# Causal products in 64-token blocks, traded halves, and a new list of steps in a linear-attention and Fourier-mixing kernel

## The chip, the core and the metric

The kernel runs on one core of a Trainium2 chip. A core has five engines that run side by side and meet through semaphores: TensorE (PE, matrix products; its weight loads are listed apart as PEld), VectorE (DVE), ScalarE (ACT), GpSimd (POOL) and SyncE (SP), which here issues most DMA transfers. TensorE writes its results to PSUM; the other operands live in SBUF. The metric is the device time of one execution in microseconds; lower is better.

## What is computed

The first part is a gated linear recurrence, for 4 batches of 8 heads, 768 tokens, 48 channels; the second mixes with Fourier transforms and then applies a normalised two-layer network.

```python
f = 1.0 / (1.0 + np.exp(-f_logit))
for t in range(S):
    state = f[:, :, t, :, None] * state + np.einsum('bhd,bhe->bhde', k[:, :, t], v[:, :, t])
    y[:, :, t] = np.einsum('bhd,bhde->bhe', q[:, :, t], state)
...
x = y.transpose(0, 2, 1, 3).reshape(B, S, H * D)
u = x + real(fft(fft(x, axis=1), axis=2))
un = (u - mean(u)) / sqrt(var(u) + 1e-06)
out = u + relu(un @ w_ch1) @ w_ch2
```

Shapes: q, k, v, f_logit are 4 x 8 x 768 x 48; w_ch1 is 384 x 1536, w_ch2 1536 x 384; the output is 4 x 768 x 384.

## The kernel before, in words

**Units.** Two heads of one batch make a unit; there are 16 units, four to a batch. A unit's tiles hold the channels of its two heads on partitions 0 to 47 and 64 to 111, and the 768 tokens along the free side, in six chunks of 128. `attention(u, ...)` is a generator, and each of its steps ends in a `yield`:

1. ScalarE makes the softplus of the gate (L331, L332).
2. VectorE scans it into a running, chunk-wise sum W (L338) and takes the chunk ends (L339); POOL copies one column (L340).
3. ScalarE makes exp(-W) into g, exp(W) into W and the decay of a chunk (L343 to L346).
4. VectorE multiplies q by g (L350) and k into W (L351).
5. TensorE makes the scores of each chunk, 128 keys by 128 queries (`sc`, L362): 24 matmuls, keys in halves of 64 on the two column halves of the array, heads on its two row halves.
6. VectorE copies the causal part of the scores from PSUM into `at` (COPY_PREDICATED, L369), in two halves.
7. In `outputs`: TensorE transposes the weighted keys of five chunks (`st`, L507), ScalarE copies them to kT (L509).
8. TensorE makes the state that each chunk adds (`ds`, L518).
9. VectorE scans the states along the chunks (L526).
10. TensorE multiplies values and scores into y (L538): 12 matmuls with 128 keys as rows, 128 queries wide.
11. TensorE adds what the earlier state gives (L545): ten matmuls. ScalarE copies y into yT in five pieces (L554 to L558).
12. TensorE transposes back (`yt`, L565) and ScalarE copies both heads into x (L567).
13. `fold` prepares the Fourier sums of the batch (L591 to L614), on VectorE and POOL.

**The second part.** When a batch's four units are through, `fnet(b)` makes the Fourier transforms on TensorE (`z` L652, `mix` L671), and `projected(b)` the network: `up` (L752) with w_ch1, ScalarE's ReLU (L754), then products with w_ch2 (`fx`, `fz`, L775), for the first pair of chunks of the first batch a plain product (`po`, L761). The weights are given in 64-bit words; ScalarE, VectorE (L241, L242) and POOL (L243) turn 24 blocks of them into fp32, which is the step `C`, after a load `r`. Near the end `judge` (L824 to L834), the step `M`, forms a flag on VectorE and TensorE that says whether a slower, exact second pass is needed; every engine loads the flag and branches on it. Here the second pass isn't taken.

**What sets the order.** The program is issued in exactly the order of a string of 684 words, `ORDER`. A number is the next step of that unit; F, P and H are steps of the second part by batch; L a load, D a few filler matmuls that write into spare PSUM (`busy`, L154), V and c a second look at the weights for the flag, W a rearrangement of w_ch2, G a memset of a tile's gap rows. Each engine executes its share strictly in that order.

**Buffers.** g and k have three tiles each that units use in turn, q four; W, kT, yT have two. PSUM has one y tile of two banks, two tiles of two banks for scores, transposes and states (`ps_a`), and two of one bank for the second part (`ps_f`).

Of the kernel before, what the change touches and what calls it, by code (L numbers as in the profile page):

```python
# [12 lines left out]
C = 128  # L13
# [5 lines left out]
X_MIN = -24.0  # L19

# [7 lines left out]
    "Gq2 r I D Gq0 L0f Gk1 L1f D Gk0 L0q i D Gq3 C Gq1 Z L0k 0 D 1 Gk2 0 L1q 1 L1k D D D D D D D D D D D "  # L28
    "D 0 0 1 0 r 1 L2f 0 2 C L1v 1 L3fk 1 3 L0v 0 1 L2q 2 0 0 r 1 L2k 3 1 0 2 r 3 L3q 2 L2v 0 C L3v C "
    "L4fk R 4 2 2 3 1 0 C 2 4 1 3 L5qv D L4qv L5fk 3 D D 3 2 0 2 3 2 3 C r 4 1 4 L6fk C r 2 5 4 L6qv 4 2 "  # L30
    "1 5 6 3 4 D 4 C 5 3 T 3 6 4 5 5 4 2 r L7fk 5 2 D L7qv 3 3 5 7 S L8fk C 4 7 6 6 5 F0 5 r r F0 F0 F0 "
    "7 4 C F0 L9fk 5 6 8 H0 H0 6 5 6 r H0 C L8qv 6 7 L9qv P0 6 7 r C P0 7 7 C 9 P0 r r 5 8 C r C F0 r 7 "
    "F0 6 P0 5 9 C 6 7 P0 r C P0 8 8 C P0 r r 7 P0 P0 8 9 H0 C P0 P0 8 7 8 C P0 H0 7 9 6 H0 H0 C 9 r C "
    "P0 9 L10fk r 9 P0 r C 9 L11fk 10 C 6 6 P0 11 4 P0 P0 P0 P0 P0 P0 10 P0 P0 P0 L10qv P0 P0 7 7 F1 9 "
    "P0 F1 H0 9 W P0 P0 P0 11 F1 P0 L11qv P0 P0 P0 9 P0 P0 P0 8 L12fk P0 11 11 8 P0 P0 10 11 F1 P0 11 11 "
    "10 L14fk F1 8 P0 14 F1 P0 10 P0 8 10 P0 P0 H1 H1 10 L12qv P0 P0 10 P0 F1 P0 11 11 10 P0 10 H1 P0 P0 "
    "P0 P0 12 12 12 P0 P0 12 P0 H1 P0 12 P0 H1 L13fk P1 P1 P1 P1 P1 14 13 P1 12 8 8 P1 P1 12 9 10 L13qv "
    "13 P1 P1 L14qv 9 P1 12 11 P1 H1 11 10 P1 P1 13 P1 13 P1 12 P1 P1 14 P1 14 V 13 P1 c V 10 10 P1 P1 "
    "P1 P1 P1 V L15fk P1 13 P1 11 V P1 P1 P1 P1 c P1 11 11 F2 V c F2 F2 H1 13 H1 F2 c 14 P1 c V c P1 P1 "
    "12 P1 P1 14 P1 P1 13 V V V P1 15 F2 c P1 12 P1 P1 P1 P1 c P1 H2 14 15 V V P1 P1 P1 P1 P1 13 P1 14 "  # L40
    "F2 P1 c P1 P1 15 V 13 P1 H2 P1 P1 L15qv P1 14 13 P1 V 12 H2 F2 14 P2 P2 P2 P2 P2 P2 P2 15 P2 P2 P2 "
    "c c 12 H2 V H2 15 H2 15 P2 c P2 15 P2 P2 15 P2 14 13 15 P2 P2 14 P2 P2 15 13 P2 P2 P2 P2 P2 H2 V 15 "
    "P2 P2 14 14 15 H2 P2 P2 P2 P2 15 15 F3 F3 P2 F3 F3 P2 F3 c P2 P2 P2 P2 P2 V P2 c P2 V c c V P2 P2 "
    "P2 P2 P2 c P2 F3 F3 P2 V P2 H3 P2 P2 P2 H3 H3 P2 P2 P2 P2 P2 P2 P2 P2 P2 P2 P3 H3 c P3 P3 P3 P3 V "
    "P3 c P3 P3 P3 c V V c P3 P3 P3 H3 P3 P3 P3 P3 P3 P3 c P3 P3 V P3 H3 P3 P3 P3 P3 P3 P3 H3 H3 P3 P3 "
    "P3 P3 P3 P3 P3 P3 P3 P3 P3 P3 V P3 P3 P3 P3 P3 c P3 c P3 P3 P3 M P3 P3 P3 P3 P3 P3 P3 P3 P3 P3 P3 "
    "P3"
# [7 lines left out]
def kernel(  # L55
# [40 lines left out]
    both = ps_y.tile([128, 2, 512], F32, tag="y", name="y").rearrange("p a b -> p (a b)")  # L96

    y_out, spare = both[:, :S], both[:, S:S + 2 * C]
# [6 lines left out]
    g_t = [fixed([128, S], f"g{i}") for i in range(3)]  # L105
    k_t = [fixed([128, S], f"k{i}") for i in range(3)]
    q_t = [fixed([128, S], f"q{i}") for i in range(4)]
    at_t = [fixed([128, 2, NCH, C], f"at{i}") for i in range(2)]
# [21 lines left out]
    def gap(*tiles):  # L130
        for t in tiles:
            nc.vector.memset(t[32:64], 0.0)

    def start():
# [6 lines left out]
        nc.gpsimd.memset(eps, 1e-6)  # L141
        nc.gpsimd.memset(two, 2.0)
        for t in te_t:
            nc.gpsimd.memset(t, 0.0)
        nc.gpsimd.memset(causal, 1.0)
        nc.gpsimd.affine_select(out=causal, in_=causal, pattern=[[1, C]], compare_op=ALU.is_ge, fill=0.0,
                                base=0, channel_multiplier=-1)

    started = []

    def busy():

        for _ in range(4):
# [823 lines left out]
```

## Time and profile before

| what | value |
|---|---|
| runs | 552.45, 552.56, 554.12 us; median 552.56 |
| profiled execution, first to last instruction | 551.2 us |
| mean granted TensorE clock | 0.982 |
| TensorE's last matmul begins | 544.7 us |
| first `z` matmul begins | 66.3 us |
| fp32 passes of one unit: sc, y at L538, y at L545, ds | 48, 24, 20, 20 |
| COPY_PREDICATED, 32 of 768 elements | 31.3 us on VectorE |
| scan at L338, 16 of them | 28.4 us on VectorE |

The timed runs lie about 1.4 us above the profiled span (552.56 against 551.2); a profiled span runs from the first to the last recorded instruction. Busy time is not the whole of an engine's load: matmul passes overlap each other in the array, so the mean duration of one is its latency, and the distance between starts is what it costs.

### The profile page before, as it was taken

What the parts mean: (1) busy time and instruction counts of PE and PEld (TensorE: products, weight loads), DVE (VectorE), ACT (ScalarE), POOL (GpSimd) and SP (SyncE); (2) the same over time, 40 slices, a digit from 0 to 9 for tenths busy, and PEclk for the clock granted to TensorE, in tenths of its full rate; (3) what the DMA queues carried; (4) which work ended last, traced back from release to release, by engine and by line L of the source; (5) the groups of instructions that cost most, each with busy time, mean ns of one, the idle gap of its engine ahead of it and who ended that gap; (6) DMA issues with size and microseconds to landing.
All of it is one profiled execution on the core that took longest, in us unless ns stands there. A gap on an engine that the chain in (4) does not pass through costs nothing.

```text
span 551.2 us, 10204 instructions
## 1 busy us (share of the span) xinstructions
PE 527.8 (96%) x4186; PEld 463.6 (84%) x4186; DVE 300.1 (54%) x534; ACT 192.8 (35%) x497; POOL 96.1 (17%) x147
## 2 busy tenths in 40 slices
PE   7797989999999999999999999999999999999995
PEld 5686768876898889889889899899889798989985
DVE  8999999984936437426644344444452441413231
ACT  5767485771332432551340422321411303021110
POOL 7146535434001000121101001003001000010000
PEclk9888799999999999999999999999999999999999
DMA  8979745353102100412540301002012004000001
GB/s 220 260 212 227 210 136 165 122 175 107 51 0 73 44 1 7 111 44 84 160 115 17 114 1 59 29 1 87 0 30 87 1 14 159 0 30 0 30 2 34
DMA packets 18398, 44.38 MB, mean 81 GB/s; under 512 B 3109, under 2 KB 4710, under 8 KB 18342
## 3 DMA queue, kind: packets, MB, share of 16 engines
q1 hardware_dynamic: 17094, 39.89, 25.9%
q0 software_dynamic: 1104, 3.54, 1.8%
q8 instruction: 35, 0.57, 0.4%
q10 hardware_dynamic: 144, 0.20, 0.1%
q14 instruction: 21, 0.17, 0.1%
HBM read 38.90 MB, written 4.72 MB: 79 GB/s over the span
## 4 chain that ended last, share of the span: by engine, by line
PE 88%; DVE 3%; ACT 3%; DMA 2%; POOL 1%; issue 1%; SPq 0%; ACTq 0%; POOLq 0%
PE up L752 35%; PE fx L775 16%; PE fz L775 12%; PE y L538 4%; PE sc L362 3%; PE z L652 3%; PE y L545 3%; PE po L761 3%; PE mix L671 3%; PE ds L518 2%; PE yt L565 2%; PE st L507 1%; PE pt L710 1%; DMA k<-in_qkf_dram 1%; DMA g<-in_qkf_dram 1%
## 5 line engine op out<-in xcount | busy, mean ns | idle before, releaser
L752 PE MATMUL up<-unT,w 128*128 128x256 f32 x864 | 197.0, 382 | 1.5 <-DVE x L730 0.9
L752 PEld LDWEIGHTS up<-unT,w 128*128 128x128 f32 x864 | 161.0, 190 | 26.1 <-issue 1.5
L754 ACT ACTIVATE h<-up 128x256 f32<-128x256 f32 x144 | 55.2, 383 | 199.4 <-PE up L752 199.4
L619 POOL DMA_INDIRECT out_dram<-x,place x16 | 16.9, 1056 | 270.4 <-DVE x L805 234.0
L775 PE MATMUL fx<-block,h 128*128 128x192 f32 x264 | 46.5, 326 | 0.0
L775 PE MATMUL fx<-w,h 128*128 128x192 f32 x264 | 44.9, 327 | 0.1
L775 PEld LDWEIGHTS fx<-w,h 128*128 128x128 f32 x264 | 43.1, 190 | 0.8 <-ACT h L754 0.4
L775 PEld LDWEIGHTS fx<-block,h 128*128 128x128 f32 x264 | 43.5, 190 | 0.0
L782 DVE TENSOR_TENSOR s<-h,h 128x768 f32<-128x768 f32 x11 | 10.5, 954 | 50.3 <-ACT h L754 50.3
L243 POOL TENSOR_TENSOR w<-w,raw 128x384 uint32<-128x384 uint32 x24 | 28.2, 1178 | 45.8 <-ACT raw L239 25.6
L369 DVE COPY_PREDICATED at<-causal,sc 128x768 f32<-128x768 uint32 x32 | 31.3, 1031 | 0.9 <-PE sc L362 0.8
L362 PE MATMUL sc<-q,W 48*64 48x128 f32 x768 | 26.3, 283 | 5.2 <-issue 3.3
L362 PEld LDWEIGHTS sc<-q,W 48*64 48x64 f32 x768 | 22.1, 138 | 8.9 <-issue 5.4
L338 DVE TENSOR_TENSOR_SCAN W<-g,bound 112x768 f32<-112x768 f32 x16 | 28.4, 1775 | 0.8 <-issue 0.7
L727 DVE TENSOR_TENSOR x<-mix,x 128x384 f32<-128x384 f32 x12 | 6.7, 555 | 39.0 <-PE mix L671 39.0
L538 PE MATMUL y<-at,v 128*64 128x128 f32 (+1 forms) x384 | 27.9, 300 | 0.0
L538 PEld LDWEIGHTS y<-at,v 128*64 128x64 f32 (+1 forms) x384 | 23.9, 143 | 3.2 <-issue 3.2
L775 PE MATMUL fz<-w,s 128*128 128x192 f32 x132 | 23.5, 328 | 0.0
L775 PE MATMUL fz<-block,h 128*128 128x192 f32 x132 | 23.5, 328 | 0.0
L775 PE MATMUL fz<-w,h 128*128 128x192 f32 x132 | 23.4, 327 | 0.0
L775 PEld LDWEIGHTS fz<-w,s 128*128 128x128 f32 x132 | 21.6, 190 | 0.3 <-issue 0.3
L697 ACT ACTIVATE rstd<-mv,eps 128x1 f32<-128x1 f32 (+1 forms) x20 | 5.9, 294 | 45.7 <-DVE mv L694 45.7
(145 smaller groups left out, 750.3 us busy)
## 6 DMA issues: line engine op xcount, KB each, us to landing
raw<-in_w_ch_dram SPq DMA_DIRECT2D x24, 384.0 KB, 4.3
g<-in_qkf_dram SPq DMA_DIRECT2D x32, 144.0 KB, 4.4
q<-in_qkf_dram SPq DMA_DIRECT2D x32, 144.0 KB, 4.1
k<-in_qkf_dram SPq DMA_DIRECT2D x32, 144.0 KB, 4.7
v<-in_v_dram SPq DMA_DIRECT2D x16, 288.0 KB, 5.0
k<-in_w_ch_dram SPq DMA_DIRECT2D x12, 384.0 KB
g<-in_w_ch_dram SPq DMA_DIRECT2D x12, 384.0 KB, 5.2
out_dram<-x SPq DMA_DIRECT2D x4, 168.0 KB
```

The costliest lines, as they stand in the source:

```text
L243: nc.gpsimd.tensor_tensor(bits, bits, lo, ALU.add)
L338: nc.vector.tensor_tensor_scan(W, g, bound[:R], 0.0, ALU.add, ALU.min)
L362: nc.tensor.matmul(ps[64 * s:64 * s + 64, r, i * C:(i + 1) * C], lhsT=W[ROWS[r], o + 64 * s:o + 64 * s + 64], rhs=Q[ROWS[r], o:o + C], sta ...
L369: nc.vector.copy_predicated(AT[:, :, half], causal.bitcast(U32).unsqueeze(1).unsqueeze(1).to_broadcast([128, 2, NCH // 2, C]), ps[:, :, :N ...
L538: nc.tensor.matmul(y[FILL[r], c * C:(c + 1) * C], lhsT=vt[:, c, r * D:r * D + (64 if r == 0 else D)], rhs=AT[:, r, c], start=(c % 4 == 0), ...
L545: nc.tensor.matmul(y[ROWS[r], c * C:(c + 1) * C], lhsT=st[ROWS[r], :, c - 1], rhs=Q[ROWS[r], c * C:(c + 1) * C], start=False, stop=True, s ...
L619: nc.gpsimd.indirect_dma_start(out=out.rearrange("b s d -> (b s) d"), out_offset=bass.IndirectOffsetOnAxis(ap=place[:, b, i:i + 1], axis=0 ...
L652: nc.tensor.matmul(z[:, cols], lhsT=src[:, j, lo:hi], rhs=tab[:, t, T % 2, cols], start=(i == 0), stop=(i == len(parts) - 1), skip_group_c ...
L671: nc.tensor.matmul(mix[:, o], lhsT=zz[:rows_of[T], T, PLACES[c]], rhs=cd[:rows_of[T], T, :NQ - odd], start=(i == 0), stop=(i == 1))
L752: nc.tensor.matmul(pp[:, :256], lhsT=w1[:, kt, m * 128:(m + 1) * 128], rhs=unT[:, kt], start=(kt == 0), stop=(kt == 2))
L754: nc.scalar.activation(hs[-1][:, m % H].rearrange("p t n -> p (t n)"), pp[:, :256], AF.Relu)
L775: nc.tensor.matmul(out, lhsT=h[:, m], rhs=blocks[i][:, m], start=(start and m == 0), stop=(m == H - 1), skip_group_check=True)
```

## The change

Scores are no longer made as 128 x 128 blocks. A chunk's causal products are split into 64-token blocks: `own`, the two diagonal blocks (each key half with its own queries), and `far`, the first key half with the second half's queries, which needs no mask. The masked copy covers the diagonal blocks alone, in one instruction; ScalarE copies `far`. The weighted keys go into g instead of W, so g lives longer and has four tiles instead of three, and the gap rows of k are set to 2^20 so that the product in the gap stays usable for the next unit. For chunks 3 to 5 the two key halves change places (in `swap`, and in the load of v, now three transfers), and for chunks 0 to 2 the two heads change places in y (`into`), so that matmuls that follow each other take the four quadrants of the array and write to different banks. y lies in two banks, three chunks in each. The keys' transposes become a step of their own, `K`. The value products come in three parts: the second diagonal block before `far`, the other two before the states. The list of steps is new.

```diff
-    y_out, spare = both[:, :S], both[:, S:S + 2 * C]
+    y_out = ps_y.tile([128, 2, 512], F32, tag="y", name="y")
+    spare = y_out[:, 0, 3 * C:]
...
-    g_t = [fixed([128, S], f"g{i}") for i in range(3)]
+    g_t = [fixed([128, S], f"g{i}") for i in range(4)]
...
-    at_t = [fixed([128, 2, NCH, C], f"at{i}") for i in range(2)]
+    at_t = [fixed([128, 2, NCH, 64], f"at{i}") for i in range(2)]
+    ao_t = [fixed([128, 2, NCH // 2, 64], f"ao{i}") for i in range(2)]
...
-        for _ in range(4):
-            nc.tensor.matmul(spare, lhsT=bound[:, :C], rhs=bound[:, :2 * C], start=not started, stop=True,
+        for _ in range(8):
+            nc.tensor.matmul(spare, lhsT=bound[:, :C], rhs=bound[:, :C], start=not started, stop=True,
...
+                nc.sync.dma_start(out=v_of[u][:, :3], in_=v[b, hp, :, :3])
+                for s in range(2):
+                    nc.sync.dma_start(out=v_of[u][64 * s:64 * s + 64, 3:],
+                                      in_=v[b, hp, 64 - 64 * s:128 - 64 * s, 3:])
...
-        nc.vector.tensor_tensor(W, W, K, ALU.mult)
-        yield
-
-        scores = []
-        for h in range(2):
-            ps = ps_a.tile([128, 2, 512], F32, tag="sc", name=f"sc{u}_{h}")
...
-                        nc.tensor.matmul(ps[64 * s:64 * s + 64, r, i * C:(i + 1) * C],
-                                         lhsT=W[ROWS[r], o + 64 * s:o + 64 * s + 64],
-                                         rhs=Q[ROWS[r], o:o + C], start=True, stop=True)
...
+        swap = lambda a: a[:, 3 * C:].rearrange("p (c s t) -> p c s t", c=3, s=2)
+        nc.vector.tensor_tensor(g[:, :3 * C], W[:, :3 * C], K[:, :3 * C], ALU.mult)
+        nc.vector.tensor_tensor(swap(g)[:, :, ::-1], swap(W), swap(K), ALU.mult)
+        yield
+
+        own = ps_a.tile([128, 2, 512], F32, tag="sc", name=f"sc{u}_0")
+        for c in range(NCH):
+            for s in range(2):
+                o, k = c * C + 64 * s, c * C + (64 * s if c < 3 else 64 - 64 * s)
+                for r in range(2):
+                    nc.tensor.matmul(own[64 * s:64 * s + 64, r, c * 64:c * 64 + 64], lhsT=g[ROWS[r], o:o + 64],
+                                     rhs=Q[ROWS[r], k:k + 64], start=True, stop=True)
+        yield
+
+        nc.vector.copy_predicated(
+            AT, causal[:, :64].bitcast(U32).unsqueeze(1).unsqueeze(1).to_broadcast([128, 2, NCH, 64]),
+            own[:, :, :NCH * 64].rearrange("p r (c t) -> p r c t", t=64))
...
+        into = lambda c, r: 1 - r if c < 3 else r
+        def values(c, r, rows, t, weights):
...
+            nc.tensor.matmul(y[FILL[g], c // 3, c % 3 * C + t.start:c % 3 * C + t.stop],
+                             lhsT=vf[rows, o:o + (64 if g == 0 else D)], rhs=weights,
+                             start=new, stop=True, skip_group_check=True)
...
+            halves(hi, lo, hi, lambda p, r, c: own[p, r, c])
+            ps = ps_a.tile([128, 2, 512], F32, tag="sc", name=f"sc{u}_1")
...
+            nc.scalar.copy(far, ps[:, :, :NCH // 2 * 64].rearrange("p r (c t) -> p r c t", t=64))
+            yield
...
+            halves(lo, hi, hi, lambda p, r, c: far[p, r, c % 3])
+            halves(lo, hi, lo, lambda p, r, c: own[p, r, c])
...
-        for c in range(1, NCH):
-            for r in range(2):
-                nc.tensor.matmul(y[ROWS[r], c * C:(c + 1) * C], lhsT=st[ROWS[r], :, c - 1],
+        for c, r in ((1, 0), (4, 1), (4, 0), (1, 1), (2, 0), (3, 1), (3, 0), (2, 1), (5, 0), (5, 1)):
+            nc.tensor.matmul(y[ROWS[into(c, r)], c // 3, c % 3 * C:c % 3 * C + C], lhsT=st[ROWS[r], :, c - 1],
...
-        nc.scalar.copy(
-            x[:, :, hp * 2 * D:(hp + 1) * 2 * D].rearrange("t c (r e) -> t c r e", r=2),
-            ps[:, :NCH * 128].rearrange("t (c r k) -> t c r k", r=2, k=64)[:, :, :, :D])
+        nc.scalar.copy(x_to[:, :3], heads[:, :3, ::-1])
+        nc.scalar.copy(x_to[:, 3:], heads[:, 3:])
```

In the list, the first F0 stood behind 153 words and stands behind 136; before it came nine C and now seven, and units 6 and 7, which had done four and two steps there, have not begun. The last word before was the last P3, with M twelve words ahead of it; now M is the last word.

```diff
-    "P3 P3 P3 P3 P3 P3 P3 P3 P3 P3 V P3 P3 P3 P3 P3 c P3 c P3 P3 P3 M P3 P3 P3 P3 P3 P3 P3 P3 P3 P3 P3 "
-    "P3"
+    "P3 P3 V P3 P3 P3 P3 P3 P3 P3 c c P3 P3 P3 P3 V P3 P3 P3 P3 P3 P3 P3 P3 c P3 P3 P3 P3 P3 P3 M"
```

## The prediction

> **What bounds the kernel now.** I read the page first, then the clock of the core, the busy time by stretch, TensorE's groups by shape, the chain of waits, and last the order in which TensorE's and VectorE's instructions stand in both programs.
>
> ```profile
> span 551.2 us, 10204 instructions
> ...
> PE 527.8 (96%) x4186; PEld 463.6 (84%) x4186; DVE 300.1 (54%) x534; ACT 192.8 (35%) x497; POOL 96.1 (17%) x147
> ...
> DVE  8999999984936437426644344444452441413231
> ...
> DMA  8979745353102100412540301002012004000001
> ...
> PE 88%; DVE 3%; ACT 3%; DMA 2%; POOL 1%; issue 1%; SPq 0%; ACTq 0%; POOLq 0%
> ```
>
> 88% of the chain is TensorE, but the DVE row says that the first ninth or more of the run is another stage: its tenths are 9 for eight slices of 13.8 us. The stretches, cut where the first `z` matmul starts (66.31), where the last weight word is converted on VectorE (123.6) and at TensorE's last matmul (545.1), make it sharp:
>
> ```profile
> 0.00:66.31 66.31, 53.51 (x766) 45.27 (x766) 61.09 (x88) 41.41 (x81) 32.94 (x65) 0.87 0.87 225
> 66.31:123.60 57.29, 54.85 (x585) 43.70 (x585) 53.90 (x91) 41.17 (x107) 26.15 (x28) 1.00 0.53 155
> 123.60:545.10 421.50, 419.41 (x2837) 374.66 (x2835) 184.59 (x358) 110.19 (x311) 36.99 (x55) 1.00 0.16 48
> 545.10:551.20 6.10, 0.00 (x0) 0.00 (x0) 0.52 (x1) 0.00 (x0) 0.00 (x0) 0.79 0.22 74
> ```
>
> Columns: stretch, length, PE, PEld, DVE, ACT, POOL busy, granted clock, DMA share, GB/s. Stage one: VectorE busy 61.1 of 66.3 us, loads 0.87 of the DMA engines. Stage two: VectorE 53.9 of 57.3 and TensorE 54.9, both full. Stage three: TensorE alone. Then 6.1 us of tail. Of stage three's matmuls the change touches these:
>
> ```profile
> L538 PE MATMUL y<-at,v 128*64 128x128 f32 x192 | 27.6, 300 | 0.0
> L538 PE MATMUL y<-at,v 128*48 128x128 f32 x192 | 27.4, 299 | 0.0
> L362 PE MATMUL sc<-q,W 48*64 48x128 f32 x768 | 26.3, 283 | 5.2 <-issue 3.3 <-DVE at L369 1.3 <-PE yt L565 0.4
> ...
> L545 PE MATMUL y<-q,stt 48*48 48x128 f32 x320 | 21.4, 277 | 0.0
> ```
>
> Every fp32 matmul shows as two passes, so x768 is 384 matmuls. The mean of one is its latency; what counts is the rhythm of starts:
>
> ```profile
> 184.43 0.38 PE L752 MATMUL up<-unT,w 128*128 128x256 f32 x1
> 184.74 1.54 PE L362 MATMUL sc<-q,W 48*64 48x128 f32 x48
> 186.21 0.48 PE L752 MATMUL up<-unT,w 128*128 128x256 f32 x1
> ```
>
> One unit's 48 `sc` passes own 1.47 us. The single start times inside show four passes beginning within 20 ns, one per quadrant of the array, and the next four 109 ns later: 12 x 0.109 = 1.31, and 0.16 goes into entering and leaving the small mode. The `up` burst behind it takes 1.49 us for 6 passes instead of 1.30, another 0.19 for coming back. Read the same way, `y` at L538 runs in twos (12 x 0.109 + 0.15 = 1.45), `y` at L545 also in twos (10 x 0.109 + 0.16 = 1.27), `ds` takes 0.78.
>
> **What the skill says.** (1) "TensorEngine Tiling (Array Packing)", Key Properties: changing the tiling mode drains the engine, and tiles load and multiply in parallel. The trace agrees: 0.16 + 0.19 us per excursion, four starts in 20 ns. (2) "TensorE: Matmul & The Clock Gate", LDWEIGHTS: the load takes its columns / 1.2 ns, 53 ns for 64. In `ds` (48 moving columns) the two column groups run independently, one start every 45 ns with 48 weight columns and every 58 ns with 64: the weight load sets the pace, plus 5 ns. (3) The same page, "Wait — 56ns, not 53.3ns?": starts never average closer than about 25 ns however short the matmul. The trace neither shows nor excludes that: `sc` averages 27 ns, `ds` 25. In favour of the change: TensorE's sequencer stood in a wait until 27.97 us and reached its next wait at 28.72, and handed over 48 passes between them, 15.7 ns each.
>
> **The change, part by part.** *Causal products.* Before, 24 `sc` + 12 `y` matmuls of 128 columns. After, per unit: 24 `own`, 12 `far` and 36 value matmuls of 64 columns, all in quadrants. No row shows such a pass. Bounds for a group of four: 56 ns (streaming, half of 109 plus the fixed part) and 109 ns (no gain from halving). I take 60: the 58 of `ds`, with the sequencer's 4 x 15.7 = 63 behind a partly filled queue. *Between chunks (L545).* "Halves traded" puts heads of chunks 0 to 2 on the other column group, so ten matmuls run in fours and a last two: 6 x 0.109 = 0.65 for 1.09. Quadrants running in fours at 128 columns are exactly what `sc` shows, so this has one answer.
>
> I count by the two orders from the first `z` on. Before: 240 sc x 0.0545 + 132 y x 0.109 + 110 y x 0.109 = 39.5 us. After: 240 own + 396 value + 132 far = 768 x 0.030 = 23.0, plus 120 x 0.0654 = 7.8, plus 10 more `ds` 0.6: 31.5. Gain 8.0. Mode changes: before 44 in x 0.163, 45 out x 0.19, 2 between small modes x 0.15 (80 ns drain and a 53 ns load laid bare) = 16.0; after 34, 33 and 13 (values to `ds`): 13.8. Gain 2.2. `up`, `fx`, `fz`, `z`, `mix`, `po` keep their counts and shapes. Together TensorE's work from the first `z` falls by **10.2 us**.
>
> *VectorE.* One COPY_PREDICATED of 768 elements (1.03 us) per unit instead of two; W*k (1.05) becomes two halves of about 0.55. Up to the subtraction that feeds the first `z`, summing mean durations in issue order gives 64.5 us before and 52.6 after: 12 predicated copies become 5 (-7.2), one scan fewer (-1.8), two weight blocks later (-2.0), the rest small. Up to the last weight word 120.7 and 108.1: 20 copies become 9 (-11.3). In the trace these points fall at 65.3 and 123.6, so sum and clock agree. Against it: in the first 20 us the new order has fewer fillers, and VectorE stands behind `own` and behind the exponentials; I charge 2.5 us. The first `z` starts at 66.3 - 11.9 + 2.5 = 57, and stage two keeps its length, since work of both engines there falls together. Loads: about 10.7 MB have to be in by then (six units of 1.18, seven blocks of 0.39, tables), at 225 GB/s 48 us plus 4.5 to landing, so they fit with 5 us to spare; `v` in three transfers instead of one costs SP two issues of 0.4 us per unit on a queue that is not full.
>
> *ScalarE.* A `far` copy (384 elements, 0.49 by the `unT` row) and heads copied in two (0.64 becomes 2 x 0.40): 0.65 us per unit. ACT's sum at the first `z` is 43 us, beneath VectorE's 53, so it is hidden; but the second value step waits for the `far` copy, and in the new order often only 0.7 us of TensorE work lies between, against 0.1 + 0.49 + 0.1, with a 0.38 `h` activation perhaps ahead of it. TensorE and all queued there wait: nothing to 0.5 us for each of 11 units; I take 2 us. The one y tile is held longer, from the first value step to the last yT copy (1.5 us); from the seventh unit on 2.7 to 15 us of TensorE work lies between, so no cost; were that cover gone, each unit would wait up to 1.5. A fourth g tile costs POOL one more memset (0.73) ahead of `bound`, which is then ready near 4.6 us, before the first scan at about 6. Keys' transposes as an own step are the same five instructions; filler matmuls, half as long and twice as many, sit where TensorE idles; the kept gap value changes no instruction.
>
> *The tail.* The judging step moves from twelve steps ahead of the end to the very end. Before, its flag was there at 526.3, and the end was set by ScalarE's last store, its flag load (0.48) and 2.45 us from its branch to its next instruction. After, from TensorE's last matmul: 0.6 the last sum, 0.98 six small VectorE instructions, 0.45 the matmul, 0.45 two more: flag at +2.5. Then POOL's flag load and branch 0.63, 2.6 until it goes on, 2.46 for its closing instructions (1.47 of it one drain), 0.8 teardown: 9.0 instead of 6.2, **+2.8**. If the drain isn't fixed, +1; at least 0.
>
> Sum: -9.3 (start) - 10.2 + 2.0 + 2.8 = -14.7 on a span of 551.2. The median of the runs lies 1.4 above the span: 552.6 - 14.7 = **538 us**.
>
> **Rivals.** *Start-up doesn't move as far:* loads or the order's latency hold the first `z` at 64 to 65. For it, DMA at 0.87; against it, VectorE was the fuller one. 538 + 7.5 = 545.5. *Better than the sum:* the tail hidden, no waits for `far`, no filler lack: 538 - 2.8 - 2.0 - 2.5 = 531. *The other side:* short passes don't start faster than the long ones, because a floor of about 25 ns per start, or weight loads of two quadrants in turn, holds a group of four at 109 ns. Then 768 x 0.0245 = +18.8: 557 us, slower. It decides from a group of 98 ns on (14.7 / 768 = 0.019 per matmul). Against it stand the sequencer's 15.7 ns and the independent rhythms in `ds`. *The change doesn't do what it says* (values not in four quadrants, banks in conflict): L545 already shows two row groups writing one bank on different partitions without delay; it would give about 550.
>
> **Chances.** The sum 0.58, start-up held 0.17, better 0.14, slower 0.08, about even 0.03. The range 529 to 548 holds the first three with their spread. A measurement tells about 0.3% (1.7 us): faster 0.90, same 0.02, slower 0.08.
>
> **What would show it.** `own` bursts of 48 passes at about 0.9 us, L545's successor at 0.8; a first `z` near 57; the last weight block near 113; the stretch from the first `z` to the last matmul about 8 us shorter than 478.8; a tail of 9. It is wrong if groups of four come every 100 ns, if the first `z` stays near 65, or if TensorE shows new idle time in stage three.

## The result, and the profile after

The changed kernel takes 549.12 us (median of 8 runs, 542.71 to 549.97), the kernel before 552.91 in the same series: a ratio of 0.9896, 95% interval 0.9858 to 0.9933. It is faster by 1%, where 2.6% had been forecast. The runs of the changed kernel lie in two groups, three at 542.7 to 544.4 us and five at 548.8 to 550.0; the profiled run, 549.43 us with a span of 547.7, belongs to the second.

From the page of the changed kernel: span, TensorE's row, VectorE's, the clock's and the DMA engines' tenths in 40 slices, and the shares of the chain that ended last.

```profile
span 547.7 us, 12758 instructions
...
PE 516.5 (94%) x5422; PEld 456.8 (83%) x5422; DVE 292.4 (53%) x534; ACT 200.3 (37%) x529; POOL 99.2 (18%) x149
...
DVE  7859889996754265564354356143264730514141
...
PEclk9888599999999999999999999999999999999997
DMA  7994657776100301213010323202010021120101
...
PE 70%; DVE 5%; POOL 1%; DMA 1%; issue 1%; ACT 0%; DVEq 0%; POOLq 0%
```

TensorE makes 5422 passes instead of 4186. Its share of the chain, 70% against 88% before, can't be compared: this chain could be followed back only to 111.9 us, the one before to 0.8. VectorE's row, which began with an 8 and seven 9s, now holds a 7, an 8 and a 5 in its first three slices, and the clock's row three 8s and a 5 in its first five. The stretches of the changed kernel, cut at the same events as before (first `z` at 65.02, last weight word on VectorE at 125.4, TensorE's last product at 537.32; columns: length, then busy time of PE, PEld, DVE, ACT, POOL, granted clock, DMA share, GB/s):

```profile
0.00:65.02 65.02, 51.67 (x1170) 44.34 (x1171) 51.41 (x79) 40.45 (x83) 29.52 (x60) 0.80 0.79 186
65.02:125.40 60.38, 56.02 (x937) 44.65 (x936) 56.50 (x95) 44.32 (x117) 26.89 (x31) 0.99 0.71 191
125.40:537.32 411.92, 408.46 (x3316) 367.72 (x3315) 182.71 (x353) 115.52 (x330) 42.77 (x59) 1.00 0.16 50
537.32:547.70 10.38, 0.38 (x2) 0.09 (x2) 1.77 (x9) 0.00 (x0) 0.00 (x0) 0.67 0.14 47
```

Start-up is where the gain is missing. VectorE's busy time fell by 9.7 us (61.09 to 51.41), but the stretch became only 1.3 us shorter, because VectorE's time without work rose from 5.2 (66.31 - 61.09) to 13.6 (65.02 - 51.41). TensorE has 1170 matmul passes in it instead of 766, at a clock of 0.80 instead of 0.87. What VectorE waited for in this stretch:

```profile
DVE stt L573 <- PE ds L565: 3.5, 1, 3.5
DVE q L359 <- ACT g L352: 2.1, 1, 2.1
DVE at L374 <- PE sc L370: 1.9, 3, 1.0
```

(Total us, times, longest.) In the kernel before no gap in front of VectorE was longer than 0.84 us from 2 us to the first `z`; its longest there:

```profile
DVE eo L593 <- POOL eo L591: 0.8, 1, 0.8
```

The three gaps of the changed kernel lie at 26.4 to 29.9, 35.7 to 37.8 and, for the longest of the third, 40.5 to 41.5 us.

The short passes themselves behave. A burst in the steady part of the changed kernel (start, length, passes):

```profile
195.23 0.57 PE L528 MATMUL y<-at,v 64*48 64x64 f32 x24
195.60 0.55 PE L545 MATMUL sc<-q,g 48*64 48x64 f32 x24
195.95 0.90 PE L370 MATMUL sc<-q,g 48*64 48x64 f32 x48
```

From start to start 24 passes take 0.37 and 0.35 us: 6 groups of four at about 60 ns.

### The profile page after: what moved, and what is told of

It reads as the page before. It is cut to its first block, busy times and chain, and to the rows that moved or that the text cites. A ratio compares the mean times of both kernels' runs of the same rounds, so it can differ in the third digit from the quotient of the medians.

```text
span 547.7 us, 12758 instructions
## 1 busy us (share of the span) xinstructions
PE 516.5 (94%) x5422; PEld 456.8 (83%) x5422; DVE 292.4 (53%) x534; ACT 200.3 (37%) x529; POOL 99.2 (18%) x149
## 4 chain that ended last, share of the span: by engine, by line
PE 70%; DVE 5%; POOL 1%; DMA 1%; issue 1%; ACT 0%; DVEq 0%; POOLq 0%
PE up L791 29%; PE fx L814 16%; PE fz L814 12%; PE z L691 3%; PE mix L710 2%; PE y L528 2%; PE pt L749 1%; PE y L582 1%; DMA raw<-in_w_ch_dram 1%; PE yt L602 1%; PE po L800 1%; PE ds L565 1%; PE sc L370 1%; PE st L507 1%; DVE w L251 1%
## 5 line engine op out<-in xcount | busy, mean ns | idle before, releaser
L374 DVE COPY_PREDICATED at<-causal,sc 128x768 f32<-128x768 uint32 x16 | 16.6, 1040 | 18.8 <-PE sc L370 18.6
L750 ACT COPY unT<-pt 128x384 f32<-128x384 f32 x24 | 11.5, 483 | 30.3 <-PE pt L749 30.3
L528 PE MATMUL y<-at,v 64*48 64x64 f32 (+1 forms) x768 | 19.6, 235 | 2.5 <-DVE at L374 1.5
L359 DVE TENSOR_TENSOR q<-q,g 112x768 f32<-112x768 f32 x16 | 16.9, 1054 | 9.5 <-ACT g L352 9.5
L814 PEld LDWEIGHTS fz<-block,h 128*128 128x128 f32 x132 | 21.7, 190 | 0.3 <-PE fx L814 0.3
L349 POOL COPY deep<-W 112x1 f32<-112x1 f32 x16 | 5.5, 344 | 89.7 <-DVE W L347 89.7
L814 PEld LDWEIGHTS fz<-w,h 128*128 128x128 f32 x132 | 21.7, 190 | 0.0
L814 PEld LDWEIGHTS fz<-w,s 128*128 128x128 f32 x132 | 21.7, 190 | 0.0
```

The lines of the kernel that those rows point to most:

```text
L359: nc.vector.tensor_tensor(Q, Q, g, ALU.mult)
L374: nc.vector.copy_predicated(AT, causal[:, :64].bitcast(U32).unsqueeze(1).unsqueeze(1).to_broadcast([128, 2, NCH, 64]), own[:, :, :NCH * 64 ...
L528: nc.tensor.matmul(y[FILL[g], c // 3, c % 3 * C + t.start:c % 3 * C + t.stop], lhsT=vf[rows, o:o + (64 if g == 0 else D)], rhs=weights, st ...
L750: nc.scalar.copy(turned[j][:, :, t], pt[:, :DM].rearrange("p (k t) -> p k t", k=3))
L814: nc.tensor.matmul(out, lhsT=h[:, m], rhs=blocks[i][:, m], start=(start and m == 0), stop=(m == H - 1), skip_group_check=True)
```

## Experiments

Three places were open: the tail (10.4 us, before 6.2), the start-up, and what makes VectorE wait there. Theories for the wait: the loads (v in three transfers with smaller packets), the clock (half for 27 us before 66 instead of 17), the fetching of TensorE's instructions, and the order with its one y tile.

| kernel | median us | ratio to before, 95% interval | first z | VectorE without work before it |
|---|---|---|---|---|
| changed | 549.12 | 0.9858 to 0.9933 | 65.0 | 13.6 |
| e1 judge early | 549.93 | 0.9905 to 0.9946 | 65.8 | 14.4 |
| e2 v in one transfer | 550.54 | 0.9927 to 0.9964 | 67.8 | 16.7 |
| e3 more filler | 548.82 | 0.9881 to 0.9935 | 65.7 | 14.7 |
| e4 fewer filler instructions | 549.10 | 0.9897 to 0.9944 | 65.2 | 13.7 |
| e5 long products, units 0 to 3 | 550.03 | 0.9909 to 0.9959 | 64.0 | 7.5 |
| e6 before, small fillers | 553.96 | 0.9989 to 1.0025 | 67.3 | 6.3 |
| e7 judge among up | 545.59 | 0.9804 to 0.9885 | 64.7 | 13.7 |
| e8 fewer loads | 549.38 | 0.9899 to 0.9949 | 66.5 | 15.6 |
| e9 fewer value passes | 547.31 | 0.9875 to 0.9918 | 61.5 | 9.3 |
| e10 long products and judge | 547.06 | 0.9863 to 0.9910 | 65.6 | 8.7 |
| e11 judge, filler at 18 us | 547.44 | 0.9836 to 0.9893 | 61.8 | 10.8 |
| e12 judge, long products in two units | 542.97 | 0.9764 to 0.9810 | 62.3 | 9.5 |
| e13 before, halved in four units | 559.50 | 1.0086 to 1.0155 | 68.8 | 7.8 |
| e14 before, halved in all | 560.28 | 1.0080 to 1.0149 | 77.3 | 12.2 |

The last two columns are from the profiled run of each, the medians from all its runs (4 to 22); in the kernel before they are 66.3 and 5.2. The kernels were timed in several series, in which the kernel before took 552.7 to 555.0 us, so kernels of different series are compared by the ratio. One profile tells the start-up to about 1 us: the changed kernel, e1 and e7 have the same list up to the first `z`, which begins at 65.0, 65.8 and 64.7.

### The tail: e1 and e7

e1 moves M right behind the last `c`, the size step of the look at the weights:

```diff
-P3 P3 P3 c P3 P3 P3 P3 P3 P3 M
+P3 P3 P3 c M P3 P3 P3 P3 P3 P3
```

> The changed kernel with the judging step M put right behind the last size step, ahead of the last six steps of the last network, instead of at the very end. Theory (the tail after the last matmul is set by the flag and the engines' jump behind it): the 10.4 us from TensorE's last matmul to the end fall to 6 to 7, as in the kernel before (6.2), and the time falls by 3.5 to 4 us, with the first z where it was (65.0). Rival (the tail is the stores and the closing work of the engines, whatever M does): within 1 us of the changed kernel.

The tail fell to 6.3 us, as the theory had it, and the time stayed. TensorE lost it ahead of the end: its stretch from the first `z` to the last product is 477.1 us long instead of 472.3. Its waits from 500 us on in e1:

```profile
PE turned L870 <- DVE most L868: 2.7, 1, 2.7
PE fz L814 <- DVE most L871: 0.4, 1, 0.4
```

Behind them the granted clock was at half from 531.6 to 535.0 us. The judging matmul waits for six VectorE instructions, which stand behind the size step and behind sums that need TensorE's own last products. So e7 puts all of it among `up` matmuls, whose results go to ScalarE:

```diff
-V P3 P3 P3 P3 P3 P3 P3 c c P3 P3 P3 P3 V P3 P3 P3 P3 P3 P3 P3 P3 c P3 P3 P3 P3 P3 P3 M
+V V P3 P3 P3 P3 P3 P3 P3 c c P3 P3 c P3 P3 P3 P3 M P3 P3 P3 P3 P3 P3 P3 P3 P3 P3 P3 P3
```

> The changed kernel with the last load and size step eight steps earlier and the judging step twelve steps ahead of the end, as far from it as in the kernel before, among matmuls with w_ch1, whose results go to ScalarE. Theory (judging early costs TensorE only where VectorE is needed by the products around it): tail near 6.3, no standstill before it, 3.5 to 4 us less than the changed kernel. Rival: TensorE stands 2 to 3 us ahead of the judging matmul here too, and the time is that of the changed kernel within 1 us.

The last stretch of e7:

```profile
538.13:544.60 6.47, 0.00 (x1) 0.00 (x0) 0.56 (x1) 0.00 (x0) 0.00 (x0) 0.84 0.21 71
```

From 500 us on TensorE's only wait is 0.2 us, and the tail is 6.5 us instead of 10.4: judging last costs the changed kernel about 4 us in its profile. The median is 3.5 us lower (545.59 to 549.12, ratios 0.9845 to 0.9896), but the intervals of the two overlap. The pair e5 and e10 below, which differ in the same edit, is 3.0 us apart (ratios 0.9934 and 0.9886), and its intervals just touch.

### Loads: e2 and e8

e2 lays v out in DRAM with the halves already traded:

```diff
-                nc.sync.dma_start(out=v_of[u][:, :3], in_=v[b, hp, :, :3])
-                for s in range(2):
-                    nc.sync.dma_start(out=v_of[u][64 * s:64 * s + 64, 3:],
-                                      in_=v[b, hp, 64 - 64 * s:128 - 64 * s, 3:])
+                nc.sync.dma_start(out=v_of[u], in_=v[b, hp])
```

> The changed kernel with v laid out in DRAM with the key halves of chunks 3 to 5 already traded, so that each unit's v is one transfer with packets of 2304 bytes instead of three with packets of 1152. Loads theory (smaller packets and two more issues per unit slow the start-up): first z from 65.0 to 61 or earlier, DMA rate in the first 40 us from about 210 to about 240 GB/s, time 3 to 4 us less. Clock, fetch and order theories: first z moves by less than 1.5 us and the time by less than 1.5 us.

The DMA rate of the first 40 us rose only from 210 to 219 GB/s, and the first `z` came later, at 67.8. e8 leaves out the loads of v for units 2 to 5, about a quarter of what is loaded before the first `z`; these units use the v of units 0 and 1:

```diff
             if name == "v":
+                if 2 <= u < 6:
+                    v_of[u] = kept[u % 2]
+                    continue
```

> The changed kernel with the loads of v for units 2 to 5 left out (2.4 MB of about 10; those units use v of units 0 and 1, so their share of the output is another). Fetch theory as to its second half (the fetches come late because the DMA engines are full): TensorE's standstills near 20.6, 33.6 and 46.6 us shrink to under half, and the first z comes 2 to 4 us earlier. Rival (the standstills are the same with freer DMA engines): they stay at 1.3 to 2 us, and the first z moves by less than 1 us.

The first standstill shrank from 1.38 to 0.17 us, the second grew to 2.48, and the first `z` came at 66.5. The loads of v as the limit are out: neither larger packets nor fewer bytes brought VectorE its work sooner. The order of the other loads was not tested; in the changed kernel ScalarE waits 1.5 us for a gate's load until 21.7 us, and VectorE 0.7 us in its wake. That full DMA engines make the standstills is not shown either.

### Clock: e3 and e11

e3 adds nine `D` words where TensorE waits between 44 and 62 us (`C 4` becomes `C D D D D 4`, the others singly or in pairs ahead of `3`, `5`, `K4`, `K5`).

> The changed kernel with nine more filler groups between 44 and 62 us, where TensorE waits for VectorE ahead of own, inter and the keys' transposes. Clock theory (TensorE's gaps bring the granted clock to half, and the half clock delays what VectorE waits for): the half clock of 49.3 to 66.4 shrinks to at most 7 us and the first z comes 2 to 4 us earlier. Loads, fetch and order theories: the clock may rise, but the first z stays within 1 us of 65.0, since VectorE is busy 0.85 of that stretch anyway.

The half clock from 49.3 to 66.4 us was gone; in the 66 us it fell from 27 to 10 us. The first stretch of e3:

```profile
0.00:65.69 65.69, 50.25 (x1242) 44.09 (x1243) 51.01 (x79) 40.21 (x83) 29.10 (x59) 0.92 0.75 184
```

Clock 0.92 instead of 0.80, first `z` no earlier. There VectorE is full, and a slow TensorE costs nothing. But from 23.2 to 30.1 us the clock was at half in e3 too, and there VectorE waits for TensorE. e11, on top of e7, adds three `D` words at that place:

```diff
-1 2 L1v D 3 0 K1
+1 2 L1v D D D D 3 0 K1
```

> The kernel with the early judging (last load and size step eight steps earlier, judging twelve steps ahead of the end) and three more filler groups between the own products of unit 1 and the inter-chunk products of unit 0, near 20 us. Clock theory for the first large gap of VectorE (26 to 30 us; it is there in all profiles whose clock is at half for 3.4 us or more between 22 and 30, and small where it isn't): the clock stays full until 33 us, the gap shrinks from 3.9 to under 2 us, first z 1 to 2 us earlier than 64.7. Rival (that gap is the number of passes ahead of ds): the gap stays over 3 us, or grows by the 1.3 us of the fillers, whatever the clock.

The clock stayed full until 47 us, and the first `z` came at 61.8, 3.0 us earlier than in e7. The gap named in the expectation shrank less than the theory said, from 3.9 to 2.8 us; the later ones at 36 and 41 us shrank from 2.9 to 1.5 together. So the fillers there are worth some 3 us of start-up in these two profiles. Not all of that need be the clock: a standstill of TensorE near 33 us, of a kind that the next runs deal with, was 0.3 us long in e11 and 1.8 in e7. The time didn't follow (547.44 against 545.59, with overlapping intervals): in the profiled run the stretch from the first `z` to the last product took 478.4 us instead of 473.4. At its place, TensorE's timeline in e11:

```profile
121.63 0.67 PE L565 MATMUL ds<-v,kT 128*64 128x48 f32 x15
125.15 0.41 PE L565 MATMUL ds<-v,kT 128*48 128x48 f32 x5 [2.86 <-issue]
```

A burst of 20 passes breaks off for 2.86 us and goes on; "issue" means that it waited for nothing that the profile shows. The clock then fell to half from 125.9 to 129.3. What such a break is, the next runs show.

### Instructions: e4, e6, e5, e9, e13, e14

The changed kernel breaks off in the same way, between two passes of one burst that have the same operands ready:

```profile
20.25 0.46 PE L582 MATMUL y<-q,stt 48*48 48x128 f32 x4
22.09 0.68 PE L582 MATMUL y<-q,stt 48*48 48x128 f32 x8 [1.38 <-issue]
```

Queue q8 of the DMA part carries instructions, 44 packets of 16 KB in the changed kernel and 35 in the kernel before. They fit TensorE's program: its 10,844 and 8,372 records (weight loads and passes) in groups of 256 would make 42 and 33. One packet was moved from 19.2 to 20.5 us, 1.56 us before the burst went on. e4 makes the filler groups of fewer instructions:

```diff
-        for _ in range(8):
-            nc.tensor.matmul(spare, lhsT=bound[:, :C], rhs=bound[:, :C], start=not started, stop=True,
+        for _ in range(2):
+            nc.tensor.matmul(spare, lhsT=bound.bitcast(F32)[:, :C], rhs=bound.bitcast(F32)[:, :C],
+                             start=not started, stop=True,
```

> The changed kernel with each filler group as two fp32 matmuls of 128 columns instead of eight bf16 ones: about the same TensorE time, half of the fillers' instructions (some 100 fewer before 13 us). Fetch theory (TensorE's instruction fetches, 16 KB for about 256 instructions, come late when the DMA engines are full, and TensorE stands in the middle of bursts at 20.7, 33.6 and 47 us): these standstills move later or vanish, the half clock behind the first one vanishes with it, and the first z moves by 1 to 3 us, probably earlier. Loads and order theories: the first z stays within 1 us of 65.0.

The first `z` stayed (65.2), so as a cure it failed, but the break moved, to another instruction of the program:

```profile
17.91 0.61 PE L566 MATMUL ds<-v,kT 128*64 128x48 f32 x13
19.91 0.46 PE L566 MATMUL ds<-v,kT 128*64 128x48 f32 x7 [1.40 <-issue]
```

The clock was full until 37.7 us here, and VectorE's gap at 26 us shrank to 0.6 and 1.1 us in two pieces; but a break of 3.2 us at 33.8 us is followed by gaps of 1.4 and 3.0 us, at 36.9 and 39.0.

That gave the means to test it. Counting TensorE's records up to a break, and looking for the instruction packet ahead of it, for ten of the breaks in the first 50 us:

```
kernel    record (mod 256)   stands from..to    after the packet's end
changed   698 (186)          20.71..22.09       1.56
changed   1205 (181)         33.55..34.88       1.56
e2        954 (186)          28.29..29.55       1.50
e4        445 (189)          18.51..19.91       1.46
e4        950 (182)          28.51..29.22       1.38
e4        1205 (181)         33.81..37.01       1.58
e7        698 (186)          20.58..22.01       1.56
e7        1459 (179)         40.27..40.87       1.53
e11       698 (186)          20.76..22.14       1.44
e11       1461 (181)         36.66..37.47       1.59
```

The breaks sit at one place modulo 256, give or take some records that are missing from a trace, and so do all others of 0.2 us or more in the first 50 us of the changed kernel, e1 to e4, e7, e8 and e11 (178 to 187). That holds whatever instruction stands there: record 698 is an inter-chunk product in the changed kernel and a filler in e11, and in e4, with fewer filler records ahead, the boundaries fall into `ds` and into the next unit's `own`. The Trainium skill ("Trainium Architecture — The Big Picture", The software stack) gives 64 bytes for an instruction; 16,384 / 64 = 256 agrees with the distance of the breaks. A break lasts until about 1.5 us after the packet of the next 256 instructions has been moved, which takes 0.9 to 1.4 us.

e6 is the counter-test with instructions where TensorE has time to spare, in the kernel before:

```diff
-        for _ in range(4):
-            nc.tensor.matmul(spare, lhsT=bound[:, :C], rhs=bound[:, :2 * C], start=not started, stop=True,
+        for _ in range(16):
+            nc.tensor.matmul(spare[:64, :64], lhsT=bound[:, :64], rhs=bound[:, :64], start=not started, stop=True,
```

> The kernel before with each filler group as sixteen bf16 matmuls of 64 weight and 64 moving columns instead of four of 128 and 256: about the same TensorE time, four times the fillers' instructions. Fetch theory: TensorE now stands in front of instruction fetches in the first 45 us, for 1 us or more at a time, each standstill ending about 1.5 us after a 16 KB fetch; the first z comes 1 to 3 us later. Rival (instruction supply doesn't limit TensorE): the first z within 0.5 us of 66.3 and no standstill that ends so.

The theory lost here: no break at such a place, VectorE's idle time up by 1.1 us, the median the same within its interval. More instructions where TensorE has time to spare do no harm. That leaves the dense bursts. e5 takes the old products for units 0 to 3, in the new list, in which only K0 to K3 move, each behind the next step of its unit:

```diff
+        if u < 4:
+            yield from long_products(u, x_all, Q, K, W, te)
+            return
         swap = lambda a: a[:, 3 * C:].rearrange("p (c s t) -> p c s t", c=3, s=2)
...
-        if te is None:
-            keys_turned(u, K)
+        if te is None or long:
+            if te is None:
+                keys_turned(u, K)
             for c in range(NCH):
```

> The changed kernel in which units 0 to 3 make their products as the kernel before did (24 sc of 128 queries, 12 value matmuls of 128 keys, two masked copies), in the new list, with v still in three transfers; a unit then has 72 fp32 passes there instead of 144, so half the instructions; units 4 to 15 are those of the changed kernel. Fetch theory (many short passes use up the fetched instructions faster than full DMA engines bring new ones): TensorE's standstills of 1.3 to 2 us at 20.7, 33.6 and 46.5 us vanish, and the first z comes at 58 to 61, although VectorE has four more masked copies (4.1 us). Order theory (the new list and the one y tile chain the units): the first z stays at 65 or comes later, by up to 4 us for the added copies, with VectorE's gaps still there.

VectorE's gaps between 20 and 45 us fell from 7.2 to 0.8 us, in nearly the new list and with the one y tile. That speaks against the order as the cause, but doesn't rule it out: VectorE's busy time rose from 51.4 to 56.5 us by the added masked copies and slower products, which fills gaps too, and the first `z` came at 64.0 only, between the two expectations. e9 keeps VectorE's and ScalarE's work and takes only value passes away:

```diff
-            halves(hi, lo, hi, lambda p, r, c: own[p, r, c])
+            if u >= 4:
+                halves(hi, lo, hi, lambda p, r, c: own[p, r, c])
...
+            else:
+                for c in range(NCH):
+                    for r in range(2):
+                        values(c, r, slice(0, C), slice(0, C), own[:, r, min(c, 4):min(c, 4) + 2])
+                for p, c in ((lo, 0), (hi, 3)):
+                    for r in range(2):
+                        values(c, r, p, hi, far[p, r, 0])
```

> The changed kernel in which units 0 to 3 form their values with 12 matmuls of 128 keys and 128 columns and 4 short ones instead of 36 short ones (the columns come from the own blocks of two chunks, so these units' share of the output is another): about the same TensorE time, the same work on VectorE, ScalarE and the DMA queues, 104 fp32 passes per unit instead of 144. Fetch theory: fewer and shorter standstills, VectorE's gaps between 20 and 42 us shrink from 8.6 to 5 us or less, and the first z comes at 60 to 62. Rival (the length of the chain from own to inter, with the one y tile, sets it): VectorE's gaps stay near 8 us and the first z within 1 us of 65.0.

First `z` at 61.5, inside the expected 60 to 62. VectorE's waits before it in e9, and the stretch:

```profile
DVE stt L582 <- PE ds L574: 3.0, 1, 3.0
DVE q L132 <- PEq L1013: 1.0, 1, 1.0
DVE at L374 <- PE sc L370: 0.8, 1, 0.8
```

```profile
0.00:61.45 61.45, 50.07 (x1011) 43.23 (x1011) 52.17 (x79) 39.90 (x83) 30.00 (x59) 0.86 0.77 196
```

The gap behind ScalarE's `g` (2.1 us) is gone; that at `ds` remains with 3.0, from 25.6 to 28.6 us, and the clock is at half from 23.6 to 27.0. No break at the boundary is left. So the largest gap needs no break: at half clock, with short passes still in front of `ds`, most of it stays. Fewer instructions are one thing that e9 changes; it also lets the first value step start later. e13 removes that doubt: the kernel before, with the same operands, waits and list, only each product of the first four units made as two halves:

```diff
+                w = C if u >= 4 else 64
+                for n in range(0, C, w):
...
-                        nc.tensor.matmul(ps[64 * s:64 * s + 64, r, i * C:(i + 1) * C],
+                            nc.tensor.matmul(ps[64 * s:64 * s + 64, r, i * C + n:i * C + n + w],
                                          lhsT=W[ROWS[r], o + 64 * s:o + 64 * s + 64],
-                                         rhs=Q[ROWS[r], o:o + C], start=True, stop=True)
+                                             rhs=Q[ROWS[r], o + n:o + n + w], start=True, stop=True)
```

> The kernel before, in which units 0 to 3 make each sc and each value matmul as two of 64 columns instead of one of 128, with the same operands, buffers, waits and list: 144 fp32 passes per unit for these two instead of 72, as the changed kernel has, at nearly the same TensorE time (a group of four at 58 instead of 2 x 54.5 per pair: sc 1.4 us instead of 1.3). Instruction theory (twice the instructions in the first units make TensorE stand for fetches and slow VectorE's chain): standstills of TensorE at indices near 185 modulo 256 of its instruction count appear before 45 us, VectorE's idle time before the first z grows from 5.2 us by 2 to 5 us, and the first z moves from 66.3 to 68 to 71. Rival (the extra instructions are free; the loss of the changed kernel comes from its order, its far step or its one y tile): the first z stays within 1 us of 66.3.

It became slower by 1.2% (559.50 us, interval 1.0086 to 1.0155). TensorE's and VectorE's waits in its first 50 us, the first break, and the stretch before the first `z`:

```profile
PE sc L364 <- issue: 4.3, 2, 3.0
...
PE y L542 <- issue: 3.0, 2, 1.6
...
DVE at L371 <- PE sc L364: 3.2, 2, 3.0
```

```profile
16.79 0.88 PE L364 MATMUL sc<-q,W 48*64 48x64 f32 x30
20.71 0.71 PE L364 MATMUL sc<-q,W 48*64 48x64 f32 x17 [3.04 <-issue]
```

```profile
0.00:68.81 68.81, 52.93 (x1054) 45.55 (x1055) 60.99 (x87) 40.93 (x80) 32.02 (x63) 0.90 0.86 214
```

Breaks at records 445, 698 and 952 (189, 186, 184 modulo 256), of 3.04, 1.58 and 1.43 us, ending 1.70, 1.58 and 1.35 us after their packets: the place modulo 256 that the breaks of the changed kernel have, in a kernel that had no break there. (The other 1.3 us of the `sc` row, ahead of 48.1 us, are no break: they stand in front of the first pass of a burst, whose W VectorE had just written, and the kernel before has 1.8 and 1.5 us of this kind, ahead of 28.0 and 44.7 us.) The first one begins at 17.67 and its packet at 17.7 us, so here the next instructions were not fetched ahead. VectorE stood from 18.9 to 22.0 us in its wake, its time without work rose by 2.6 us (5.2 to 7.8) while its busy time stayed (61.1 to 61.0), and the first `z` moved by 2.5 us to 68.8. So it is shown that TensorE breaks off for its instructions and that VectorE stands for it. How much of the 8.4 us in the changed kernel is this, no run shows: e13 has 2.6 of it. Nor is all of e13's loss in start-up: its profile is 5.1 us longer than that of the kernel before, and 2.2 of these lie between the first `z` and the last weight word, with a clock of 0.97 instead of 1.00, which stays unexplained.

e14 does the same in all units (the bound `u >= 4` becomes `u >= 16`).

> The same halving in all 16 units. Instruction theory: as with four units up to the first z; behind it the fetches are covered where bursts of short passes stand between long ones, so the stretch from the first z to the last matmul grows from 478.7 by at most 4 us (12 units times some 0.15 us of longer bursts, and a standstill here or there). If instruction supply limits TensorE there too, it grows by 8 us or more.

The median is that of e13 within 0.8 us, and the stretch behind the first `z` takes 480.5 us in its profile against 481.1 in e13: halving the other twelve units costs nothing there that can be told. Its profiled run, with the first `z` at 77.3, was its slowest (566.13 us); the first 77 us are read no further.

### The best version: e10 and e12

e10 joins e5 and e7, e12 does so with long products in units 0 and 1 alone (`if u < 2`).

> The two edits of long products in units 0 to 3 and of judging twelve steps ahead of the end together. If they add up: first z near 64, tail near 6.3, and the time of the kernel with the early judging alone or up to 1 us less. If the long products give nothing in the median, the time is 545 to 546.

> The early judging, and long products in units 0 and 1 alone, so two more masked copies on VectorE (2.1 us) than the changed kernel and half the instructions for the first two units. If the early gap comes from the short passes of units 0 and 1 and each unit pays its own share: the gap at 26 to 30 us goes, the later ones at 36 and 41 stay in part, first z 62 to 63.5 and the time 543 to 545, below both other kernels with the early judging. If VectorE's added copies eat it: first z 64 to 65.5, time 545 to 547.

e10 gives nothing over e7: four units' masked copies eat what the fewer passes bring. e12 is the fastest of all, 542.97 us, 2.1% below the kernel before; its ratio of 0.979 lies below e7's, but the two intervals overlap slightly. Its stretches:

```profile
0.00:62.34 62.34, 47.72 (x1027) 41.44 (x1027) 52.80 (x79) 39.47 (x81) 32.16 (x63) 0.86 0.74 193
62.34:122.10 59.76, 55.65 (x913) 44.12 (x913) 55.95 (x94) 43.19 (x116) 25.80 (x31) 0.97 0.69 189
122.10:536.16 414.06, 410.28 (x3346) 368.66 (x3339) 183.56 (x361) 116.38 (x331) 43.95 (x60) 1.00 0.17 50
536.16:542.70 6.54, 0.00 (x0) 0.00 (x0) 0.56 (x1) 0.00 (x0) 0.00 (x0) 0.84 0.21 70
```

The gap at 26 to 30 us is gone, VectorE's work is 52.8 us instead of 56.5 in e5, and the tail is 6.5 us. One break stays, of 1.3 us at 36.2 us in an `own` burst, and VectorE stands for 1.6 us there.

## Why the prediction was wrong, and where it was right

| term | predicted | measured |
|---|---|---|
| VectorE's work before the first `z` | -11.9 | -9.7 (61.09 to 51.41) |
| VectorE's waits before it | +2.5 | +8.4 (5.2 to 13.6) |
| first `z` begins at | 57 | 65.0 |
| first `z` to TensorE's last product | -8.2 | -6.4 (478.7 to 472.3) |
| last product to the end | 9.0 | 10.4 |

The last three rows are 8.0, 1.8 and 1.4 us off, together the 11.1 us between 538 and 549.1.

**The step that failed** is "The first `z` starts at 66.3 - 11.9 + 2.5 = 57". Of the 8.0 us that it was off, 5.9 are in the charge of 2.5 us for VectorE standing behind `own` and behind the exponentials, and 2.2 in the work (rounding apart). A first `z` near 65 is what the prediction itself named as a sign of being wrong. For the first: the 2.5 us were set down for the first 20 us, where fillers are few, and the waits came later, from 26 to 41.5 us. The working gave TensorE only its time per unit, which falls, and put the supply of its instructions and the half clock in start-up at nothing. Before the first `z` TensorE has 2341 records instead of 1533, and the clock is at half for 27 us instead of 17. e13 shows that doubling the instructions of these units alone makes the breaks and adds 2.6 us to VectorE's waits (6.8 us in the median, part of it behind the first `z`); e9, with 40 passes of 144 taken away, has the first `z` 3.6 us earlier; e11, with fillers against the half clock at 22 to 29 us, 3.0 us. The latter two overlap (both also shorten what the other does), so they are not added, and what the new order has of the rest stays open. For the second: the two halves of W*k took 0.56 and 0.69 us instead of 0.55 (7.4 us for six units instead of 6.6), q*g 1.02 instead of 0.94, and the two `xs` instructions 2.7 us instead of the 0.9 that they took before.

**An argument used the wrong way round.** The sequencer's 15.7 ns per pass was taken as proof that instructions come fast enough. It shows how fast those come that are already there. A unit's 144 passes are 288 records in some 2.5 us of bursts (0.8 + 0.4 + 0.4 + 0.9), while a break in e13 shows 3.0 us from the start of a packet to the next record, for 256.

**Stage two**, from the first `z` to the last weight word, was to keep its length and grew from 57.3 to 60.4 us: VectorE's work in it rose from 53.9 to 56.5 us. The stretch behind it shrank by 9.6 us (421.5 to 411.9).

**The rival** of a held start-up had the place right (first `z` at 64 to 65) and was 3.6 us off in time (545.5 us). Of the causes it gave, the loads of v are ruled out by e2 and e8; e5 speaks against the order, which stays possible for a part. The breaks and the half clock were not among them. That the case of short passes outside the four quadrants lay nearest in time (550) is luck: the passes do run in four quadrants.

**TensorE's part held.** Groups of four at 60 ns, `own` at 0.75 to 0.84 us a burst behind the first `z`, where about 0.9 had been said. TensorE's time without the waits fell by 9.8 us from the first `z` to its last product (474.3 to 464.5), 10.2 predicted. Its waits there rose by 3.3 (4.5 to 7.8), where 2.0 had been charged. They aren't where they were expected: none is for the `far` copy. The longest row is `pt` behind VectorE's `un`, 3.2 us. The rival in which short passes hold 109 ns is out.

**The tail** was right in kind: flag 2.4 us after the last product (2.5 said), then the engines' jump and the closing instructions; the sum is 1.4 us short. The size that was off is the jump: GpSimd's next instruction came 4.0 us after its branch (540.4 to 544.4), where 2.6 had been said.

**Left open.** Why the runs of the changed kernel lie in two groups 5.8 us apart. e11's profiled run shows that one break far behind the first `z`, with the half clock after it, comes with 5 us more in that stretch; that the groups differ by such a break was not shown, since the faster runs left no trace. Their mean clock was 0.975 to 0.980, that of the others 0.969 to 0.974, which fits less time at half clock, but tells no cause. What decides whether the next packet is fetched ahead in time is open too: e8 says that it is not simply the load on the DMA engines.

## What to carry to other kernels

When a change makes matmuls shorter and more numerous, count instructions as well as time: a stretch in which 256 instructions go by in under some 3 us can stand for the next packet, and the profile shows it only as "issue" in the middle of a burst. In the kernel before, halving the passes of the later units cost nothing that could be told behind the first `z`, where long passes stand between the bursts (e14), though a single break can come there too (e11). In start-up, where another engine waits for each burst, breaks took part of the gain; so short passes belong where nothing waits, and the first units may keep long ones, as in e12. Put a step whose matmul waits for another engine among matmuls that don't need that engine.

## What the runs showed of the hardware

- TensorE can stand at places 256 records apart in its program when bursts are dense: for 0.3 to 3.2 us, ending about 1.3 to 1.7 us after the end of a 16 KB instruction packet (the changed kernel, e2, e4, e7, e11, e13).
- The granted clock falls to half in pieces of 3.4 us (3.4, 6.8 and 17.1 us in the changed kernel), as the Trainium skill has it ("TensorE: Matmul & The Clock Gate", What's actually happening: a window of 3413 ns). One piece started at 22.0 us behind bursts of quarter-array passes with only 1.4 us of standstill; three filler groups of the whole array ahead of it (1.3 us) kept the clock full until 47.4 us (e11). In e9 a piece of half clock began at 23.6 us with no break ahead of it, behind 1.5 us in which TensorE waited for ScalarE's kT.
- Short passes in four quadrants run at 56 to 60 ns for a group of four (the bursts at 195.23 and 195.60 us of the changed kernel), so 14 to 15 ns from start to start on the average.
